# Linear attention and a feed-forward layer on one core: the seven-product second layer carried to three more groups, with a new static order

## The chip, the core and the metric

The kernel runs on one core of a Trainium2 chip. The time is the device time of one execution in microseconds (us). The engines are TensorE (PE; its weight loads are shown as PEld), VectorE (DVE), ScalarE (ACT), GpSimd (POOL) and SyncE (SP), which issues nearly all DMAs.

## What is computed

The inputs are float32: q, k and v of 8 batches, 8 heads, 576 positions and 64 columns, a 128 x 64 matrix omega, a gain of 512 and two matrices, 512 x 2048 and 2048 x 512.

```python
    scale = 1.0 / np.sqrt(np.sqrt(D))
    q_s, k_s = (q * scale, k * scale)
    def phi(x):
        proj = np.einsum('bhsd,md->bhsm', x, omega)
        sq = np.sum(x * x, axis=-1, keepdims=True) / 2.0
        h = proj - sq
        h = h - np.max(h, axis=-1, keepdims=True)
        return np.exp(h) / np.sqrt(m)
    q_p, k_p = (phi(q_s), phi(k_s))
    kv = np.einsum('bhsm,bhsd->bhmd', k_p, v)
    z = np.sum(k_p, axis=2)
    num = np.einsum('bhsm,bhmd->bhsd', q_p, kv)
    den = np.einsum('bhsm,bhm->bhs', q_p, z)[..., None] + 1e-06
    return (num / den).astype(np.float32)
...
    xn = (x - mu) / np.sqrt(var + 1e-06) * g_ln
    ch = np.maximum(xn @ w_ch1, 0.0) @ w_ch2
    return (x + ch).astype(np.float32)
```

x is that attention's result, laid out as 4608 rows (8 x 576) of 512.

## The kernel before, in words

The 4608 rows of x are 9 tiles of 512 (T), each of four chunks of 128. A float32 factor is cut into a high and a low part, so that each product is three TensorE passes (high x high, low x high, high x low). The first three tiles go through both layers in the ordinary way (`mm1`, `mm2`). The other six form three **pairs** p = 0, 1, 2, and there the first layer is done by Strassen's scheme in Winograd's form: two tiles by two blocks of 128 hidden columns take seven products instead of eight.

One pair is four **groups** (`gen_pair`). A group has two first-layer sets j (`one_set`: seven `product`, 42 matmuls of 512 columns, lines 1423 to 1425) and then the second layer of those four blocks. For pairs 0 and 1 the second layer is ordinary: eight `one_chunk`, each twelve matmuls of 512 columns (lines 1745 to 1747), whose result DVE adds into x (`drain`). For pair 2 it is two `two_chunks`, each seven `product2` of twelve matmuls of 256 columns (lines 1665 to 1667). There ACT copies and snapshots accumulators (`gen_copy`, `gen_snap`), DVE adds (`gen_x2`, `gen_y2s`) and drains by halves (`drain2`); the hidden values are first made into the seven forms A11, S3, S2, A12, S1, A22, S4, each with a low part (`form_a11` and the functions behind it, `finish`).

The seven forms of x for a pair's first layer are made by `gen_forms` (`split` writes high and low parts, `summed` the sums). They read x transposed, which `gen_flip` makes chunk by chunk by a DMA transpose: for pair 0 it goes to DRAM and back (`gen_stage`), for pairs 1 and 2 straight into one SBUF tile. The seven forms of the first weights lie in DRAM and stream through a ring of eight slots (`gen_slot`); the second weights stream through `gen_w2`, their seven forms (made by `gen_w2form`, in pair 1) through `gen_w2q_one`.

The attention's work on keys (`gen_k`, line 674), sums (`gen_sums`, line 718), queries (`gen_q`, lines 816, 833) and x (`gen_x`, line 899) is put between these matmuls as short **visits** of TensorE. The order of everything is static: while the program is built, a planner (`Plan`) with costs of its own simulates the engines and writes each engine's instructions in one fixed order. Visits are placed by the table `SLOT`, ranks shifted by `SHIFT`. In the middle layers a visit may use a pair of PSUM banks (`plan.pair`), or a second pair that is lent (`plan.loan`).

Of the kernel before, what the change touches and what calls it, by code (L numbers as in the profile page):

```python
# [23 lines left out]
P = 128  # L24
# [51 lines left out]
class Plan:  # L76
# [25 lines left out]
    def __init__(self):  # L102
# [12 lines left out]
        self.pair, self.loan, self.at, self.where = (), (), 0, 0  # L115
# [83 lines left out]
    def go_to(self, at, step):  # L199

        self.at, self.step, self.turn = at, step, 0

    def serve(self, lend):
# [11 lines left out]
        sets = (self.pair,) + (lend and len(due) > 1) * (self.loan,)  # L215
# [10 lines left out]
        if lend and len(cols) == len(todo) > 2 and guests:  # L226
# [74 lines left out]
    def run(self):  # L301
        while self.ready or self.stuck():
# [24 lines left out]
            if eng == SP:  # L327
# [6 lines left out]
                part.end = self.dma_at + (FLOWN if part.want[-1] == "flip" else 0.0)  # L334
# [12 lines left out]
def favor_ffn(ctx, tc, kT, kTr, vF, vR, qT, qD, omT, gT, w1, w2, out):  # L347
# [86 lines left out]
    def slots(pair):  # L434
        i = 512 * int(pair[0][1:])
        return all_banks.rearrange("p a b -> p (a b)")[:, i : i + H * SLOT].rearrange("p (a b) -> p a b", b=SLOT)[:, :, 0 : D + 1]

# [9 lines left out]
    n_hid, n_xnT, n_mb, n_st = names("hid", 2), names("xnT", 1), names("mb", 3), (*names("st", 3), "st3")  # L447
# [3 lines left out]
    turn = {k: names(f"turn_{k}", n) for k, n in (("k", 2), ("q", 2), ("blk", 3), ("mx", 2), ("xn", 3), ("w", 3), ("wl", 5))}  # L451
# [10 lines left out]
    plan.pair, plan.loan = b_at, b_h  # L462
# [413 lines left out]
    def gen_x(c, b_turn):  # L876
# [13 lines left out]
        t_x = yield "get", n_x  # L890
# [105 lines left out]
    def gen_flip(t, i, xn, t_n, xn_turn):  # L996
# [7 lines left out]
        if t >= NREG + 2:  # L1004
            p, u = divmod(t - NREG, 2)
            yield wait("stage", p)
            cols = slice(u * T + i * P, u * T + (i + 1) * P)
            words = stages[p][1].bitcast(U16).rearrange("p k (c b) -> p b k c", b=2)
            eng = yield either(1.27, 1.13)
            copy(eng, words[:, :, :, cols], flipped)  # L1010
            free(t_n, xn_turn, t_p)
            done(("xT", t, i))
            return
# [143 lines left out]

    n_form = ("A11", "S3", "S2", "A12", "S1", "A22", "S4")
# [6 lines left out]
    xT_away = dram.tile([P, NK, 2 * T], F32, tag="xT_away", name="xT_away", bufs=1)  # L1165
# [4 lines left out]
    hforms, fs, w2q, users, halves_left = {}, {}, {}, {}, {}  # L1170
# [61 lines left out]
    def gen_more():  # L1232
# [8 lines left out]
        extra[n_st[-1]] = more[:, 1, 0:48]  # L1241
        free(n_x[N_X + 2], n_st[-1])

    def gen_stage(p):

        if p:
            yield wait("used", 1, NF - 1)
            yield wait("formed", p - 1)
            t_s = yield "get", n_xnT
            st = tile_of(t_s, [P, NK, 2 * T])  # L1250
            stages[p] = [t_s], st
            done(("stage", p))
            return
# [9 lines left out]
        for k in range(NK):  # L1263
            plan.add(plan.cur.rank, gen_stage_k(p, k))

    def gen_stage_k(p, k):
        yield dma(P * 2 * T)
        nc.sync.dma_start(stages[p][1][k], xT_away[:, k])
# [9 lines left out]
    def gen_forms(p):  # L1278
        if p:
            for u in range(2):  # L1280
                for i in range(TC):
                    yield wait("xT", NREG + 2 * p + u, i)
        else:
            for k in range(NK):
                yield wait("xk", p, k)
# [3 lines left out]
        def cut(ap):  # L1289
            return [ap] if n_part == 1 else [ap[:, k] for k in range(2)]  # L1290
# [7 lines left out]
        def split(name, src):  # L1298
            tags, hi, lo = yield from room(name)
            for o, a in zip(cut(hi), src):  # L1300
                yield us(ACT, 0.22 + 0.00083 * 2 * T / n_part)
                nc.scalar.copy(out=o, in_=a)
            for o, a, b in zip(cut(lo), src, cut(f32(hi))):
                yield dve2(2 * T / n_part)
# [4 lines left out]
        def summed(out_, a, b, op):  # L1309
            for o, x, y in zip(out_, a, b):  # L1310
                yield dve2(2 * T / n_part)
                nc.vector.tensor_tensor(out=o, in0=x, in1=y, op=op)

        yield from split("A11", a11)
        t_s = yield "get", n_quad
        s1 = cut(tile_of(t_s, [P, 2, T]))
        yield from summed(s1, a21, a22, ALU.add)
        yield from summed(a21, a11, a21, ALU.subtract)
        yield from split("S3", a21)
        yield from summed(a11, s1, a11, ALU.subtract)  # L1320
        yield from split("S2", a11)
        yield from split("A12", a12)
        yield from split("S1", s1)
        free(t_s)
        yield from split("A22", a22)
        yield from summed(a12, a12, a11, ALU.subtract)
        yield from split("S4", a12)
        free(*stages[p][0])
        done(("formed", p))

# [34 lines left out]
    def gen_w2(p, f, t_w):  # L1365
# [6 lines left out]
        users[p, f] = 2 if p == NPAIR - 2 else 1  # L1372
        done(("w2s", p, f))

    def leave(p, f):
        users[p, f] -= 1
        if not users[p, f]:
            free(w2s[p, f][0])

    def gen_w2form(j):  # L1380
        f, g = 2 * j, 2 * j + 1
        for n in (f, g):
            yield wait("w2s", NPAIR - 2, n)
        tags = yield "get", n_big, 4
        r = [tile_of(tag, [P, DM]) for tag in tags[0:2]]
        t = [tile_of(tag, [P, 2, HALF], F32R) for tag in tags[2:4]]
        for i, n in enumerate((f, g)):
            w = f32(w2s[NPAIR - 2, n][1])
            yield dve2(DM)
# [566 lines left out]
```

## Time and profile before

| | |
|---|---|
| runs, us | 930.43, 930.6, 930.69; median 930.6 |
| profiled execution, us | 930.92 |
| its span, us | 929.2 |
| TensorE granted clock | 1.000 over the span |
| DMA | 202.71 MB, mean 218 GB/s |

In the page's parts an engine's busy time is the union of its instructions; a matmul's record lasts longer than the distance to the next one, so a busy TensorE may still issue slower than it can. The chain of work that ended last says which engine set the end. In the order's rows below, the DVE and PE instructions stand as they were written to each engine.

### The profile page before, as it was taken

The numbers are of one execution on the slowest core, as the hardware profiler recorded it, in microseconds if no ns is written. First come the engines' busy times: TensorE is split into PE (matmuls) and PEld (weight loads), VectorE is DVE, ScalarE is ACT, GpSimd is POOL, SyncE is SP. The second block draws the span as 40 slices with busy tenths as digits, with TensorE's granted clock in tenths as the row PEclk, the third lists the DMA queues.
The fourth block names the chain that finished last, engine by engine and source line by source line (L and its number), as shares of the span: only waits on it lengthen the run. The fifth ranks groups of instructions, "written<-read, shape, count | busy, mean of one in ns | idle before, by whom it ended". The sixth has DMA issues, their size and how long they took to land.

```text
span 929.2 us, 17577 instructions
## 1 busy us (share of the span) xinstructions
PE 921.2 (99%) x6871; PEld 766.9 (83%) x6871; DVE 673.6 (72%) x1178; ACT 503.1 (54%) x915; POOL 121.1 (13%) x47
## 2 busy tenths in 40 slices
PE   9999999999999999999999999999999999999998
PEld 6878777888888888888888888888888888988988
DVE  6999988674758877667566547898836596585765
ACT  7878876565753472437756444557412245253452
POOL 5001314130420041001302110304000000000000
PEclk9999999999999999999999999999999999999999
DMA  8676369996446559295956634796946558574562
GB/s 310 218 269 238 142 180 365 371 347 167 126 115 233 183 152 341 94 369 118 288 176 202 187 110 174 240 385 150 314 149 225 204 203 298 166 285 141 177 226 91
DMA packets 142577, 202.71 MB, mean 218 GB/s; under 512 B 44064, under 2 KB 79008, under 8 KB 142496
## 3 DMA queue, kind: packets, MB, share of 16 engines
q1 hardware_dynamic: 142352, 201.34, 65.6%
q8 instruction: 54, 0.88, 0.4%
q10 hardware_dynamic: 144, 0.26, 0.1%
q14 instruction: 27, 0.22, 0.1%
HBM read 140.74 MB, written 52.43 MB: 208 GB/s over the span
## 4 chain that ended last, share of the span: by engine, by line
PE 92%; DVE 6%; issue 1%; DMA 0%; SPq 0%; ACT 0%; DVEq 0%
PE b L1423 8%; PE b L1425 8%; PE b L1424 8%; PE b L1745 6%; PE b L1746 6%; PE b L1747 6%; PE b L1122 5%; PE b L1078 4%; PE b L1124 4%; PE b L1123 4%; PE b L1080 4%; PE b L1079 4%; PE b L674 4%; PE b L718 3%; PE b L899 3%; PE b L1665 3%
## 5 line engine op out<-in xcount | busy, mean ns | idle before, releaser
L845 POOL PARTITION_ALL_REDUCE quad<-quad x35 | 118.2, 3398 | 517.3 <-ACT quad L392 380.8
L1423 PE MATMUL b<-w,w 128*128 128x512 f32 x336 | 131.9, 392 | 0.0
L1425 PE MATMUL b<-w,w 128*128 128x512 f32 x336 | 130.8, 389 | 0.0
L1424 PE MATMUL b<-w,w 128*128 128x512 f32 x336 | 130.8, 389 | 0.0
L1745 PE MATMUL b<-w,w 128*128 128x512 f32 x256 | 101.2, 395 | 0.0
L1746 PE MATMUL b<-w,w 128*128 128x512 f32 x256 | 99.8, 390 | 0.0
L1747 PE MATMUL b<-w,w 128*128 128x512 f32 x256 | 99.7, 389 | 0.0
L683 ACT ACTIVATE kp<-b,mb 128x128 f32<-128x128 f32 x264 | 72.3, 389 | 26.8 <-DVE mb L677 25.9
L1122 PE MATMUL b<-w,hid 128*128 128x512 f32 x192 | 78.1, 407 | 0.0
L1078 PE MATMUL b<-xnT,w 128*128 128x512 f32 (+1 forms) x200 | 78.1, 390 | 0.0
L1080 PE MATMUL b<-xnT,w 128*128 128x512 f32 (+1 forms) x200 | 76.2, 381 | 0.0
L1079 PE MATMUL b<-xnT,w 128*128 128x512 f32 (+1 forms) x200 | 76.2, 381 | 0.0
L1124 PE MATMUL b<-w,hid 128*128 128x512 f32 x192 | 75.2, 392 | 0.8 <-DVE hid L1096 0.8
L1123 PE MATMUL b<-w,hid 128*128 128x512 f32 x192 | 75.0, 390 | 0.0
L1423 PEld LDWEIGHTS b<-w,w 128*128 128x128 f32 x336 | 63.1, 188 | 14.2 <-ACT b L1481 0.9
L1487 ACT COPY hid<-b 128x512 f32<-128x512 f32 x64 | 37.6, 587 | 68.1 <-PE b L1425 38.7
L1425 PEld LDWEIGHTS b<-w,w 128*128 128x128 f32 x336 | 63.1, 188 | 13.3
L1424 PEld LDWEIGHTS b<-w,w 128*128 128x128 f32 x336 | 63.1, 188 | 12.7
L1481 ACT COPY b<-b 128x512 f32<-128x512 f32 x32 | 18.6, 580 | 83.6 <-PE b L1425 67.8
L1494 DVE TENSOR_TENSOR b<-b,hid 128x512 f32<-128x512 f32 x32 | 22.3, 697 | 56.5 <-ACT hid L1487 56.3
L1096 DVE SCALAR_TENSOR_TENSOR hid<-b,hid 128x512 fp32r<-128x512 f32 x48 | 33.0, 688 | 37.9 <-ACT hid L1094 37.5
L1745 PEld LDWEIGHTS b<-w,w 128*128 128x128 f32 x256 | 48.0, 188 | 10.8
(220 smaller groups left out, 2050.8 us busy)
## 6 DMA issues: line engine op xcount, KB each, us to landing
w<-wf SPq DMA_DIRECT2D x168, 256.0 KB, 5.0
w<-w SPq DMA_DIRECT2D x32, 512.0 KB, 6.6
w<-w2a SPq DMA_DIRECT2D x32, 512.0 KB, 5.7
quad<-qD SPq DMA_DIRECT2D x28, 512.0 KB, 5.1
away<-x SPq DMA_DIRECT2D x33, 256.0 KB, 2.8
w2a<-w SPq DMA_DIRECT2D x16, 512.0 KB, 6.2
wf<-wide SPq DMA_DIRECT2D x32, 256.0 KB, 2.8
w2t<-wide SPq DMA_DIRECT2D x32, 256.0 KB, 3.1
```

The lines of the kernel that those rows point to most:

```text
L845: nc.gpsimd.partition_all_reduce(mx.rearrange("p a b -> p (a b)"), qc.rearrange("p a b -> p (a b)"), P, bass_isa.ReduceOp.max)
L1078: nc.tensor.matmul(ph[:, ts], w[:, 0, cs], xnT[:, 0, k, ts], start=k + i0 == 0, stop=False)
L1079: nc.tensor.matmul(ph[:, ts], w[:, 1, cs], xnT[:, 0, k, ts], start=False, stop=False)
L1080: nc.tensor.matmul(ph[:, ts], w[:, 0, cs], xnT[:, 1, k, ts], start=False, stop=k == NK - 1 and i1 == TC)
L1122: nc.tensor.matmul(accs[i][:, c], hl[:, 0, cs], w[:, 0, c], start=(f == 0), stop=False)
L1124: nc.tensor.matmul(accs[i][:, c], hl[:, 1, cs], w[:, 0, c], start=False, stop=f == NF - 1 and c == parts[-1])
L1423: nc.tensor.matmul(o, w[:, 0, cs], hi[:, k], start=first and k == 0, stop=False, skip_group_check=True)
L1424: nc.tensor.matmul(o, w[:, 1, cs], hi[:, k], start=False, stop=False, skip_group_check=True)
L1425: nc.tensor.matmul(o, w[:, 0, cs], lo[:, k], start=False, stop=k == 1, skip_group_check=True)
L1745: nc.tensor.matmul(acc[:, o], hl[:, 0, cs], w[:, 0, o], start=n == 0 and o is parts[0], stop=False)
L1746: nc.tensor.matmul(acc[:, o], hl[:, 0, cs], w[:, 1, o], start=False, stop=False)
L1747: nc.tensor.matmul(acc[:, o], hl[:, 1, cs], w[:, 0, o], start=False, stop=n == 3 and o is parts[-1])
```

## The change

Four things change together. (1) `strassen2` says that groups 1 to 3 of pair 1 (`G1` = 1) also take the seven-product second layer; all hidden forms and weight loads get the pair as an index. (2) `gen_w2form` no longer waits for pair 1's own loads of the second weights: it reads them from DRAM itself (`gen_w2in`) after chunk 19 of x. (3) x transposed goes through DRAM for all three pairs, so that the SBUF tile can hold up to eight more chunks of x (`n_room`, `lend_room`) until a pair is staged; the forms of x are made by parts that run side by side. (4) Visits in the pairs may use a third pair of banks, the two accumulators alternate over all sets (`turned`), and the tables of the static order are all new.

```diff
-        sets = (self.pair,) + (lend and len(due) > 1) * (self.loan,)
+        sets = (self.pair,) + self.where * (self.third,) + (lend and (len(due) > 1 or self.where > 0)) * (self.loan,)
...
+        if t >= ORDERED:
+            yield wait("place", c - 1)
-        t_x = yield "get", n_x
+        t_x = yield "get", n_x + n_room
...
-        if t >= NREG + 2:
-            p, u = divmod(t - NREG, 2)
-            yield wait("stage", p)
...
-            copy(eng, words[:, :, :, cols], flipped)
...
-                xT_away[:, :, u * T + i * P : u * T + (i + 1) * P], f32(whole).rearrange("p (a b) c -> p a (b c)", b=P)
+                xT_away[u // 2][:, :, u % 2 * T + i * P : u % 2 * T + (i + 1) * P], f32(whole).rearrange("p (a b) c -> p a (b c)", b=P)
...
     def gen_stage(p):
         if p:
-            yield wait("used", 1, NF - 1)
             yield wait("formed", p - 1)
-            t_s = yield "get", n_xnT
-            st = tile_of(t_s, [P, NK, 2 * T])
+            yield wait("a2b", p - 1, STAGE[p - 1][0])
+            for n in n_room:
+                yield "get", (n,)
+            for u in range(2):
+                for i in range(TC):
+                    yield wait("xT", NREG + 2 * p + u, i)
+            st = tile_of(n_xnT[0], [P, NK, 2 * T])
...
+            for k in range(NK):
+                plan.add(plan.cur.rank, gen_stage_k(p, k, st[:, k]))
...
+    def gen_stage_k(p, k, place):
+        if p:
+            yield wait("a2b", p - 1, STAGE[p - 1][k])
         yield dma(P * 2 * T)
-        nc.sync.dma_start(stages[p][1][k], xT_away[:, k])
+        nc.sync.dma_start(place, xT_away[p][:, k])
...
+        if p:
+            yield wait("a2b", p - 1, FORM_AT if p < 2 else FORM_LAST)
+        def begin(name, src):
+            plan.add(rank + n_form.index(name), split(name, src))
+        begin("A11", a11)
+        begin("A12", a12)
+        begin("A22", a22)
...
+    def strassen2(p, gr):
+        return p == NPAIR - 1 or (p == NPAIR - 2 and gr >= G1)
...
     def gen_w2form(j):
-        f, g = 2 * j, 2 * j + 1
-        for n in (f, g):
-            yield wait("w2s", NPAIR - 2, n)
+        yield wait("x", W2GO)
+        for n in (2 * j, 2 * j + 1):
+            yield wait("w2", n)
...
+        for i in range(2):
+            plan.add(plan.cur.rank, gen_w2in(2 * j + i, r[i], low[i]))
...
+    def gen_w2in(f, r, low):
+        yield dma(2 * P * DM, 0.5)
+        nc.sync.dma_start(r, w2_away[f][:, 0])
+        nc.sync.dma_start(low, w2_away[f][:, 1])
+        done(("w2in", f))
...
+    def turned():
+        other = b_acc[1 - b_acc.index(latest[0])]
+        b_c, latest[0] = latest[0], other
+        return other, b_c
...
+    def two_chunks(p, gr, h):
+        ta, j = NREG + 2 * p, NF + 2 * gr + h
+        b_a, b_d = b_acc[2:4] if h else b_at
+        b_b, b_c = turned()
...
-            if p == NPAIR - 1:
+            if strassen2(p, gr):
                 for h in range(2):
-                    yield from two_chunks(gr, h)
+                    yield from two_chunks(p, gr, h)
                 continue
...
-W2F = -30
+G1 = 1
+ORDERED = 7
+STAGE, FORM_AT, FORM_LAST = ((2, 3, 4, 5), (4, 5, 6, 6)), 7, 22
+W2GO = 19
+W2F = (240, 25)
```

`SHIFT`, `SLOT`, `EARLIER`, `WF` and some planner constants have other numbers; three places show what they and the code do to the order.

**TensorE, end of the first-layer sets of pair 1's second group.** Before (lines 1423 to 1425 are the last product of the set, 1745 to 1747 the first ordinary chunk):

```order
L1423 MATMUL b<-w_100_6139,w_10_3495 128x512
L1424 MATMUL b<-w_100_6139,w_10_3495 128x512
L1425 MATMUL b<-w_90_6140,w_10_3495 128x512
L1745 MATMUL b<-w_100_6727,w_130_6813 128x512
L1746 MATMUL b<-w_100_6727,w_130_6813 128x512
L1747 MATMUL b<-w_100_6727,w_130_6813 128x512
L1745 MATMUL b<-w_120_6734,w_150_6876 128x512
```

Of the change, at the same place (lines 1716 to 1718 are `product2`):

```order
L1460 MATMUL b<-w_100_6513,w_10_3489 128x512
L1461 MATMUL b<-w_100_6513,w_10_3489 128x512
L1462 MATMUL b<-w_90_6514,w_10_3489 128x512
L1716 MATMUL b<-w_100_7014,kp_7079 128x256
L1717 MATMUL b<-w_100_7014,kp_7079 128x256
L1718 MATMUL b<-w_100_7014,kp_7079 128x256
```

In three groups 96 matmuls of 512 columns become 168 of 256: over the program, `one_chunk` has 480 instead of 768, `product2` 1176 instead of 672.

**TensorE, the last visits.** Before, `gen_x` (line 899) stands by itself inside a first-layer set of pair 1's second group:

```order
L1424 MATMUL b<-w_50_5990,w_110_4033 128x512
L1425 MATMUL b<-w_40_5991,w_110_4033 128x512
L899 MATMUL b<-kv_5257,quad_6634 64x65 x16
L1423 MATMUL b<-w_60_6057,w_00_3410 128x512
L1424 MATMUL b<-w_60_6057,w_00_3410 128x512
```

Of the change, two `gen_x` (line 902) stand together ahead of pair 1's first group's chunks (1800 to 1802 are `one_chunk`):

```order
L1461 MATMUL b<-w_100_6513,w_20_3593 128x512
L1462 MATMUL b<-w_90_6514,w_20_3593 128x512
L902 MATMUL b<-kv_5160,quad_6630 64x65 x16
L902 MATMUL b<-kv_5160,quad_6635 64x65 x16
L1800 MATMUL b<-w_100_6582,w_130_6673 128x512
L1801 MATMUL b<-w_100_6582,w_130_6673 128x512
```

Behind the first matmul of `mm1` the order has 64 stretches of visits before and 59 now, with the same matmuls in them; the last visit is in pair 1's second group before, and in its first group now.

**DVE, end of pair 1**, where the forms of x for pair 2 are made. Before, among the chunks (1305 `split`, 1312 `summed`, 1765 `drain`, 1390 to 1402 `gen_w2form`):

```order
L1305 TENSOR_TENSOR w_40_7533<-xnT_6190,w_50_7532 128x1024
L1765 SCALAR_TENSOR_TENSOR x_6384<-b,w_150_4372,x_6384 128x512
L1312 TENSOR_TENSOR xnT_6190<-quad_7504,xnT_6190 128x2x512
L1402 TENSOR_TENSOR wide_7427<-wide_7427,wide_7566 128x512
L1390 TENSOR_TENSOR wide_7474<-w_120_7395 128x512
L1765 SCALAR_TENSOR_TENSOR w_150_4372<-b,w_150_4372 128x512
L1305 TENSOR_TENSOR w_50_7582<-xnT_6190,w_60_7581 128x1024
```

Of the change, among the two sets of `two_chunks` (1306 `split`, 1313 `summed`, 1538 `gen_x2`, 1773 `drain2`):

```order
L1773 SCALAR_TENSOR_TENSOR w_150_4353<-b,w_150_4353 128x256
L1313 TENSOR_TENSOR xnT_7437<-xnT_7437 128x2x512
L1773 SCALAR_TENSOR_TENSOR x_6729<-b,w_150_4353,x_6729 128x256
L1306 TENSOR_TENSOR w_30_8019<-xnT_7437,w_40_8018 128x1024
L1306 TENSOR_TENSOR w_60_8021<-xnT_7437,w_70_8020 128x1024
L1313 TENSOR_TENSOR xnT_7437<-wide_8024,xnT_7437 128x512
L1306 TENSOR_TENSOR w_40_8135<-xnT_7437,w_50_8134 128x1024
L1538 TENSOR_TENSOR b<-b,hid_4359 128x512
L1773 SCALAR_TENSOR_TENSOR x_6740<-b,w_150_4353,x_6740 128x256
L1313 TENSOR_TENSOR xnT_7437<-wide_8025,xnT_7437 128x512
```

The forms' DVE work now stands in front of the second set's `gen_x2`, on which TensorE waits; the weights' forms are gone from here, to earlier places.

## Rows read from the trace of the kernel before

**Rows 1.** The page: part 1, and engines of the chain in part 4.
```profile
PE 921.2 (99%) x6871; PEld 766.9 (83%) x6871; DVE 673.6 (72%) x1178; ACT 503.1 (54%) x915; POOL 121.1 (13%) x47
PE 92%; DVE 6%; issue 1%; DMA 0%; SPq 0%; ACT 0%; DVEq 0%
```
**Rows 2.** Timeline of PE (start us, us, engine, line): rows with idle before, in brackets.
```profile
39.48 0.50 PE L1124 MATMUL b<-w,hid 128*128 128x512 f32 x1 [0.29 <-DVE hid L1096]
128.15 0.49 PE L1124 MATMUL b<-w,hid 128*128 128x512 f32 x1 [0.54 <-DVE hid L1096]
151.84 0.50 PE L833 MATMUL b<-quad,om_hi 128*128 128x512 f32 x1 [0.46 <-DVE kv L746]
484.95 0.47 PE L833 MATMUL b<-quad,om_hi 128*128 128x512 f32 x1 [0.16 <-DVE x L910]
```
**Rows 3.** Windows: one second layer of pair 1, then of pair 2; columns ahead.
```profile
core 0: us, PE busy (x) PEld busy (x) DVE busy (x) ACT busy (x) POOL busy (x), PEclk, DMA share, GB/s
704.96:726.72 21.76, 21.76 (x98) 18.02 (x96) 9.86 (x17) 1.22 (x2) 0.00 (x0) 1.00 0.33 115
865.40:885.45 20.05, 20.05 (x170) 20.04 (x169) 13.77 (x28) 6.73 (x12) 0.00 (x0) 1.00 0.29 108
```
**Rows 4.** Timeline of PE: matmuls of 512 columns, then of 256.
```profile
710.17 0.39 PE L1747 MATMUL b<-w,w 128*128 128x512 f32 x1
710.40 0.39 PE L1745 MATMUL b<-w,w 128*128 128x512 f32 x1
...
870.08 0.28 PE L1665 MATMUL b<-w,w 128*128 128x256 f32 x1
870.20 0.28 PE L1666 MATMUL b<-w,w 128*128 128x256 f32 x1
```
**Rows 5.** The chain of waits, two visits (start us, us, what): double, single.
```profile
410.75 2.02 PE b L899 x64
412.76 0.43 PE b L1745
...
446.20 1.08 PE b L899 x32
447.28 0.43 PE b L1423
```
**Rows 6.** Timeline of DVE: pair 1's end, then pair 2's first second layer.
```profile
747.97 1.22 DVE L1305 TENSOR_TENSOR w<-xnT,w 128x1024 fp32r<-128x1024 f32 x1
749.11 0.74 DVE L1765 SCALAR_TENSOR_TENSOR x<-b,w,x 128x512 f32<-128x512 f32 x1
...
788.69 0.68 DVE L1606 SCALAR_TENSOR_TENSOR wide<-b,wide 128x512 f32<-128x512 f32 x1
789.29 0.68 DVE L1534 TENSOR_TENSOR quad<-wide,quad 128x512 fp32r<-128x512 f32 x1
...
798.32 0.48 DVE L1719 SCALAR_TENSOR_TENSOR w<-hid,st,w 128x256 f32<-128x256 f32 x1
798.71 0.48 DVE L1719 SCALAR_TENSOR_TENSOR w<-b,st,w 128x256 f32<-128x256 f32 x1
...
802.16 0.70 DVE L1494 TENSOR_TENSOR b<-b,hid 128x512 f32<-128x512 f32 x1 [2.19 <-ACT hid L1487]
```
**Rows 7.** Timeline of PE: the first matmul of that second layer.
```profile
786.68 0.28 PE L1665 MATMUL b<-w,kp 128*128 128x256 f32 x1
```
**Rows 8.** Windows: pair 0's first two groups, pair 1's first, a stretch early on.
```profile
388.80:440.40 51.60, 51.60 (x410) 42.81 (x409) 34.47 (x58) 27.28 (x55) 3.23 (x1) 1.00 0.79 254
440.40:498.80 58.40, 58.24 (x505) 47.68 (x504) 37.17 (x69) 38.38 (x72) 12.90 (x4) 1.00 0.68 208
593.00:642.50 49.50, 49.50 (x325) 40.46 (x324) 46.10 (x75) 31.14 (x42) 17.48 (x5) 1.00 0.85 276
139.00:209.00 70.00, 69.55 (x651) 55.78 (x651) 54.06 (x97) 44.57 (x80) 19.86 (x6) 1.00 1.08 359
```
**Rows 9.** One line's instructions: the ring's loads, L1353.
```profile
DMA to landing us min/median/max: 2.6/5.0/8.1
```

More of the change, by code (lines that the diff above doesn't have):

```diff
@@ L114, in __init__ @@
         self.mlp = None
-        self.pair, self.loan, self.at, self.where = (), (), 0, 0
+        self.pair, self.loan, self.third, self.at, self.where, self.zone = (), (), (), 0, 0, 0
         self.shared = {}
@@ L225, in serve @@
         guests = [p for p in cols if p.want[3]]
-        if lend and len(cols) == len(todo) > 2 and guests:
+        if lend and not self.where and len(cols) == len(todo) > 2 and guests:
             todo.remove(guests[0])
@@ L1475, in one_set @@
         tick(6)
-        plan.add(MOST_URGENT, form_a12(j, b_b) if wide else relu2(ta, g, bank(b_b), b_b))
+        plan.add(MOST_URGENT, form_a12(p, j, b_b) if wide else relu2(ta, g, bank(b_b), b_b))
     def gen_copy(p, j, b_a, b_b):
@@ L1544, in form_a11, with form_a22 @@
         free(b_a)
-        done(("f", j, "A11"))
-        yield from finish(j, "A11")
-    def form_a22(j, s):
-        a22 = yield from whole(j, "A22")
+        done(("f", p, j, "A11"))
+        yield from finish(p, j, "A11")
+    def form_a22(p, j, s):
+        a22 = yield from whole(p, j, "A22")
         eng = yield either(0.5, 0.34)
@@ L1595, in form_a12 @@
         )
[L1596 removed]
+        done(("hf", p, j, "A12"))
         left_b.pop()
@@ L1611, in form_s4 @@
             free(b_b)
-        done(("f", j, "S4"))
+        done(("f", p, j, "S4"))
         plan.cur.rank = MOST_URGENT
-        yield from finish(j, "S4")
+        yield from finish(p, j, "S4")
     def gen_w2q():
@@ L1659, in product2 @@
             w = w2q[t_w]
-            for i in range(2):
-                o = bank(t_b)[:, i * HALF : (i + 1) * HALF]
-                cs = slice((2 * h + i) * P, (2 * h + i + 1) * P)
-                yield us(PE, 0.36)
-                fresh, last = first and i == s == 0, s == 1
-                nc.tensor.matmul(o, hl[:, 0, cs], w[:, 0], start=fresh, stop=False, skip_group_check=True)
-                nc.tensor.matmul(o, hl[:, 0, cs], w[:, 1], start=False, stop=False, skip_group_check=True)
-                nc.tensor.matmul(o, hl[:, 1, cs], w[:, 0], start=False, stop=last, skip_group_check=True)
@@ new lines, in product2 @@
+            nc.tensor.matmul(o, hl[:, 0, cs], w[:, 0], start=fresh, stop=False, skip_group_check=True)
+            nc.tensor.matmul(o, hl[:, 0, cs], w[:, 1], start=False, stop=False, skip_group_check=True)
+            nc.tensor.matmul(o, hl[:, 1, cs], w[:, 0], start=False, stop=last, skip_group_check=True)
+            if h and i:
+                free(tag, t_w)
+    def two_chunks(p, gr, h):
+        ta, j = NREG + 2 * p, NF + 2 * gr + h
+        b_a, b_d = b_acc[2:4] if h else b_at
+        b_b, b_c = turned()
+        sk = snaps[h]
```

312 lines of the change are left out of this document (164 added, 148 removed).

## The prediction, made before the changed kernel was run

> **What bounds the kernel now.** I read the page first: TensorE is busy 99% of the span, and 92% of the chain that ended last is TensorE [rows 1]. Busy time alone would not prove it, so I then looked in the timeline for every row of TensorE with idle time before it. After the first 32 us only four waits are long enough to be marked, 0.29, 0.54, 0.46 and 0.16 us, 1.45 together [rows 2]: three for DVE on the way to hidden values, queries or a sum, one for DVE on x. The kernel is bound by the number of matmuls that TensorE issues, from 32 us to 4 us before the end. A change gains only by taking issues away, and it loses as soon as any other engine or a DMA is late.
>
> The clock is granted at 1.00, that is 2.4 GHz, in all stretches shown [rows 3, 8], and TensorE has no long pauses in which it could fall; I leave it out.
>
> **Seven products for eight.** Before, the second layer of a quiet group of pair 1 takes 21.76 us; the same work in pair 2, done with seven products, takes 20.05 us [rows 3]. Both windows run from the stage's first matmul to that of the next stage, and hold no visit. They are 96 matmuls at 0.227 us (start to start: 710.17 to 710.40) and 168 at 0.12 (870.08 to 870.20) [rows 4]. The three groups that change are of just this kind, so the term is 3 x 1.71 = **5.1 us gained**. The extra matmuls, 504 for 288, are already in it. Half as many columns take 53% of the time, not 50%, so of the eighth that is saved in columns (12.5%) 7.9% remains.
>
> Here the Trainium skill speaks another way. "TensorE: Matmul & The Clock Gate", section "Back-to-back issue gap", gives a warm gap of N/2.4 + 2.5 ns. By it the gain would be an estimated 288 x 215.8 - 504 x 109.2 ns = 7.1 us, 2 us more than by the rows; no matmul of rows 4 is that quick, so the measured windows decide.
>
> **Visits.** The order has 59 stretches of visits for 64. What a stretch costs beyond its own matmuls shows in the chain: a single `gen_x` takes 1.08 us and the matmul behind it 0.43; two in one stretch take 2.02 and again 0.43 [rows 5]. A free matmul takes 0.23 [rows 4]. Two single ones cost 2 x (1.08 + 0.20) = 2.56 us, a double one 2.02 + 0.20 = 2.22. Each joined pair saves 0.34 us, and five save **1.7 us**. The work in them is the same. Other mixes (keys beside x) save a little less, so 1.2 to 1.7.
>
> **DVE's new work.** From the order: 36 more `finish`, 18 `form_sum`, 6 each of `form_s4`, `form_a12`, `form_a22`, `gen_x2` and `gen_y2s`, 48 `drain2`; 24 `relu2` and 24 `drain` fewer. DVE issues 512 columns every 0.60 us, a `drain2` every 0.39 and 1024 columns every 1.14 us [rows 6]. With `form_a22` at a `drain2`'s price, 78 x 0.60 + 54 x 0.39 less 48 x 0.60 is about 39 us more work. It costs nothing where DVE has time: the same second layer in pair 2 leaves DVE idle 6.3 of 20 us [rows 3], and none of TensorE's waits [rows 2] lies there. Without that cover each late `gen_x2` would stop TensorE by as much as it is late.
>
> **The seam of pair 1 and 2** is where cover is thinnest. Eleven operations of 1024 columns for pair 2's forms of x (four sums, seven low parts; some cut in two) are 11 x 1.14 = 12.5 us. They had eight ordinary chunks (21.8 us) with one `drain` each; now they share 20 us with 10 us of drains and sums. I laid the DVE order out from the start of the second layer. The last set's `form_s4` starts 2.0 us after that (786.68 to 788.69) [rows 6, 7]. From there to the start of the second set's `gen_x2` stand 11 operations of 512 columns (6.6 us), 8 drains (3.1), a cast (0.3) and 4 of 1024 (4.6): it starts at +16.6 and ends at +17.3. Today its twin starts at +15.5 (802.16) [rows 6], after idling for ACT. TensorE needs it for the second set's sixth product, at 10.0 + 5 x 1.44 = +17.2. So it is some 0.1 us late. The low part of S2 then ends at about +23.9; pair 2's third product wants it at 20.05 + 2 x 1.36 + 0.45 = +23.2: another 0.7 us. **Cost 0.8 us**; bounds 0 (a tenth faster per operation) and 3 us (as much again from each of the three forms that follow).
>
> **Moved at no cost.** `gen_w2form` (eight times four operations of 512 and four of 256 columns, some 4 us each time [rows 6]) leaves pair 1, where DVE was busy 46.1 of 49.5 us in the first group [rows 8] without holding TensorE, for earlier groups. Pair 0's first two groups have DVE busy 71.6 of 110 us [rows 8]. By the order three of the eight `gen_w2form`, nine more `gen_q` steps and more of x come in, and their DVE work rises by half, to about 100 us of a stretch that visits lengthen to 117. That is 0.87, less than the 0.93 that went well. The waits of rows 2 may go or others come: I keep their 1.45 us and take 0 and twice that as bounds. The start (up to 32 us) has the same TensorE matmuls, and the last group the same instructions: nothing.
>
> **DMAs.** In: 16 stores of x transposed, 8 loads of it (512 KB), 32 `gen_w2in` and 42 loads of weight forms, 256 KB each; out: 12 `gen_w2` of 512 KB. Net some 21 MB on 203. SP takes them in order, so a store that waits for its drain holds what is queued behind it; at the end of pair 1 these are 15 stores. What must not be late are the ring's loads. They land 2.6 to 8.1 us after their issue [rows 9], and eight slots at 1.36 us a product give 10.9 us. No cost.
>
> **Sum.** 930.92 (profiled execution; span 929.2) - 5.1 - 1.7 + 0.8 = 924.9. The median of the runs stands 0.3 us below the profiled execution, so the forecast is **924.6 us**.
>
> **Rivals.**
> *DVE sets the pace* (0.10). If DVE is late not once but in each new wide group and in pair 0's full stretch, TensorE loses 0.5 to 1 us in some six places, and the gain falls to 2 or 3 us: 928. For it speaks that DVE's share in pair 0 rises to 0.87; against it that 0.93 cost nothing in pair 1 and that pair 2's groups carry the same wide work without a wait.
>
> *The DMA queue in pair 0* (0.06, slower). Counted between ring loads in SP's order, pair 0's first two groups move about 36 MB where they moved 23. The ring of weights then waits behind transposes, `gen_w2in` and stores, and TensorE's `product` waits for its slot. 36 MB in 117 us is 308 GB/s. For it: in today's first group the queue is 0.79 busy at 254 GB/s [rows 8], which at a full share would be 321. Against it: 359 GB/s were held for 70 us earlier [rows 8]. It decides below about 285 GB/s: 36 MB then take 126 us, 9 us too many, and the time is some 933. By the Trainium skill, "DMA: Bandwidth & Descriptors", section "Where 436 GB/s comes from", the core's HBM limit is about 358 GB/s; the 359 of rows 8 agree with that, and by it this rival stays out.
>
> *Weight loads bind* (0.01). Each 256-column matmul has its own weight load; the loads fill 20.04 of 20.05 us there, against 18.02 of 21.76 [rows 3]. If they could not run beside matmuls the groups would be slower than the ordinary ones, but rows 3 have that cost in them.
>
> *The order gives nothing back* (0.08). The three groups save 5.1 us, but the joined visits end on later data and their 1.7 us go into new waits: 926.5.
>
> **How the numbers follow.** The forecast has 0.75. Its own range is 922.3 (no seam, the old waits gone: 924.6 - 0.8 - 1.45) to 928.2 (seam 3 us, the waits doubled: 924.6 + 2.2 + 1.45). For 8 in 10 the range takes in most of the DVE case above and is rounded down below: 922.0 to 928.5. A change under 0.2% (1.9 us) can hardly be told from none, so "faster" ends at 928.7. The forecast, the visits case and six tenths of the DVE case lie under it, with little of the forecast's own tail beyond: 0.85. The rest of the DVE case and that tail are "same", 0.09; the DMA case is "slower", 0.06.
>
> **What would show it.** Right: the wide second layers of pair 1 at 20.0 to 20.2 us; TensorE's marked waits 1 to 3 us in all; a wait of 0.5 to 1 us in pair 2's first set, released by DVE's `split`. The visits are wrong if a joined pair still costs two times 1.28 us. The forecast falls if TensorE has waits ended by a DMA into w (the ring), if landings pass 10.9 us in pair 0, or if wide groups of pair 1 take over 21 us.

## The result and the profile after

The changed kernel took 935.52 us (median of 934.68, 935.53, 935.52 and 937.79) against 930.62: 1.0051 times as long, 95% interval 1.0039 to 1.0064. It is slower by 0.5%, where 924.6 was forecast. Measured again in rounds with the kernel before it was 934.88 to 930.97, with a ratio on record of 1.0067 (1.0040 to 1.0094); the two medians alone give 1.0042, and two long runs of the six, 940.33 and 942.15, raise the ratio. The profiled execution took 937.79 and was the slowest of the first four; its span is 936.0 us, 6.8 more than before.

The page's part 1 and the engines of the chain [rows 1 before]:

```profile
PE 920.0 (98%) x7087; PEld 775.0 (83%) x7087; DVE 706.8 (76%) x1278; ACT 522.7 (56%) x959; POOL 118.2 (13%) x47
PE 84%; DVE 10%; ACT 2%; DMA 2%; issue 1%; SPq 0%; DVEq 0%; ACTq 0%
```

TensorE has fallen from 92% to 84% of the chain; DVE has risen from 6% to 10%, ACT and DMA from 0% to 2% each. The windows, with columns as in rows 3: the first and the third wide second layer of pair 1; two short stretches; the two stretches of time of pair 0 that rows 8 show; and pair 0's first two groups as they lie in the changed kernel:

```profile
675.46:695.50 20.04, 20.04 (x169) 20.03 (x168) 13.76 (x28) 6.72 (x12) 0.00 (x0) 1.00 0.34 124
...
753.92:774.25 20.33, 20.33 (x170) 20.15 (x168) 20.30 (x36) 12.00 (x18) 0.00 (x0) 1.00 0.58 208
...
471.46:474.87 3.41, 3.41 (x35) 2.92 (x32) 2.35 (x9) 0.00 (x0) 3.05 (x1) 0.50 1.03 414
522.66:526.07 3.41, 3.41 (x9) 2.67 (x8) 1.27 (x2) 0.73 (x2) 0.00 (x0) 0.50 1.09 298
388.80:440.40 51.60, 51.60 (x514) 42.81 (x514) 43.31 (x73) 30.44 (x64) 9.64 (x3) 1.00 1.01 335
440.40:498.80 58.40, 56.08 (x545) 45.95 (x543) 47.18 (x92) 37.74 (x66) 14.24 (x5) 0.97 0.94 283
...
387.20:516.69 129.49, 126.93 (x1205) 104.20 (x1204) 108.57 (x194) 82.93 (x151) 33.51 (x10) 0.99 0.97 293
```

The seven products are worth nearly what was said: 20.04 us, 20.33 in the third group, for 21.76 [rows 3]. But twice the granted clock is 0.50, that is 1.2 GHz, for 3.41 us, about half of which, 1.7 us, is lost each time; before, it was 1.00 in every stretch read. In the two stretches of rows 8 the DMA engines are busy 1.01 and 0.94 of the time, for 0.79 and 0.68. Pair 0's first two groups now last 129.5 us, where the prediction had 117; over them DVE is busy 0.84 of the time, and the DMA engines 0.97 at 293 GB/s. TensorE's waits, summed by the pair of lines (us in total, times, longest):

```profile
PE b L1460 <- ACT b L1525: 2.3, 1, 2.3
PE b L902 <- ACT quad L392: 1.8, 1, 1.8
...
PE b L1460 <- ACT hid L1531: 1.1, 1, 1.1
PE b L674 <- DVE x L913: 1.0, 2, 0.6
PE b L674 <- ACT kp L683: 0.9, 1, 0.9
PE b L1115 <- ACT hid L1087: 0.7, 1, 0.7
PE b L1117 <- DVE hid L1089: 0.6, 2, 0.3
PE b L718 <- ACT quad L392: 0.5, 1, 0.5
```

With two short ones (L1462 0.3, L833 0.2) that is 9.4 us behind the first 32 us, where four waits of 1.45 us in all stood [rows 2]; the three longest end on ACT. The timeline of PE at those three, called the three stops below, with the first matmuls at the halved clock, and at the seam of pair 1 and 2:

```profile
471.18 1.80 PE L902 MATMUL b<-kv,quad 128*64 128x65 f32 x32 [1.77 <-ACT quad L392]
472.91 0.80 PE L1460 MATMUL b<-w,w 128*128 128x512 f32 x1
...
521.87 0.50 PE L1460 MATMUL b<-w,w 128*128 128x512 f32 x1 [2.29 <-ACT b L1525]
522.20 0.39 PE L1461 MATMUL b<-w,w 128*128 128x512 f32 x1
522.43 0.43 PE L1462 MATMUL b<-w,w 128*128 128x512 f32 x1
522.67 0.63 PE L1460 MATMUL b<-w,w 128*128 128x512 f32 x1
...
617.27 0.50 PE L1460 MATMUL b<-w,w 128*128 128x512 f32 x1 [1.14 <-ACT hid L1531]
...
777.91 0.50 PE L1462 MATMUL b<-w,w 128*128 128x512 f32 x1 [0.29 <-DVE w L1306]
```

And the timeline of ACT there, which says why ACT was late:

```profile
467.22 1.05 ACT L1003 COPY wide<-wide 128x1024 uint16<-128x1024 uint16 x1 [1.87 <-DMA xTa<-wide]
468.17 0.59 ACT L1554 ACTIVATE w<-b 128x512 fp32r<-128x512 f32 x1
468.66 0.59 ACT L1525 COPY b<-b 128x512 f32<-128x512 f32 x1
469.17 1.05 ACT L853 ACTIVATE quad<-quad 128x1024 f32<-128x1024 f32 x1
470.13 1.00 ACT L392 COPY quad<-b 128x1024 f32<-128x1024 f32 x1
...
513.87 1.09 ACT L1003 COPY wide<-wide 128x1024 uint16<-128x1024 uint16 x1
519.04 1.05 ACT L1003 COPY wide<-wide 128x1024 uint16<-128x1024 uint16 x1 [4.09 <-DMA w2t<-wide]
520.00 1.34 ACT L392 COPY wide<-wide 128x1024 uint16<-128x1024 uint16 x1
521.19 0.62 ACT L1525 COPY b<-b 128x512 f32<-128x512 f32 x1
...
616.03 0.72 ACT L986 ACTIVATE wide<-w,w 128x512 f32<-128x512 f32 x1 [2.23 <-DMA w2t<-wide]
616.66 0.56 ACT L1531 COPY hid<-b 128x512 f32<-128x512 f32 x1
```

At 513.87 ACT starts the word split (`gen_flip`, L1003) of one chunk, and then comes to the next chunk's. Its output goes into one of eight `wide` buffers, whose last user is a store of the second weights' forms (`w2t<-wide`) that has not landed. ACT sits idle for 4.09 us. Two places behind the word split stands `gen_copy` (L1525), for which TensorE waits 2.29 us. The other two places read the same way, one with a store of x transposed (`xTa<-wide`). By the Trainium skill, "PSUM — Partial Sum Buffer", section "Engine vs sequencer instructions", the queues of ScalarE, VectorE and GpSimd are strict FIFO; the rows of ACT agree. The page's part 6 has the store's landing, before and after (KB, median us):

```profile
w2t<-wide SPq DMA_DIRECT2D x32, 256.0 KB, 3.1
```
```profile
w2t<-wide SPq DMA_DIRECT2D x32, 256.0 KB, 5.2
```

**Where the time went.** I took each matmul's distance to the next start in the timeline and subtracted what that pair of shapes takes when nothing waits. What is left over, TensorE's lost time, is 12.2 us before and 26.2 after. So issuing changed by 936.0 - 929.2 - 14.0 = -7.2 us, near the forecast's -6.8, and 14.0 us of stalls ate it twice over: 5.7 us in the three stops (1.96, 2.45, 1.30 from start to start), 3.4 in the clock behind two of them, 4.9 in some ten smaller ones. The count depends somewhat on what is taken as free: with the median distance of each pair of shapes in these traces the rise is 13 us, and issuing fell by some 6 us.

### The profile page after: what moved, and what is told of

The parts are those of the page before. It is cut to its first block, busy times and chain, and to the rows that moved or that the text cites. A ratio compares the mean times of both kernels' runs of the same rounds, so it can differ in the third digit from the quotient of the medians.

```text
span 936.0 us, 18335 instructions
## 1 busy us (share of the span) xinstructions
PE 920.0 (98%) x7087; PEld 775.0 (83%) x7087; DVE 706.8 (76%) x1278; ACT 522.7 (56%) x959; POOL 118.2 (13%) x47
## 2 busy tenths in 40 slices
DMA packets 164567, 224.28 MB, mean 240 GB/s; under 512 B 45568, under 2 KB 95360, under 8 KB 164480
## 4 chain that ended last, share of the span: by engine, by line
PE 84%; DVE 10%; ACT 2%; DMA 2%; issue 1%; SPq 0%; DVEq 0%; ACTq 0%
PE b L1460 8%; PE b L1462 8%; PE b L1461 8%; PE b L1071 5%; PE b L1115 4%; PE b L1718 4%; PE b L1717 4%; PE b L1716 4%; PE b L1117 4%; PE b L1116 4%; PE b L1072 4%; PE b L1073 4%; PE b L718 4%; PE b L674 4%; PE b L1800 3%; PE b L902 3%
## 5 line engine op out<-in xcount | busy, mean ns | idle before, releaser
L845 POOL PARTITION_ALL_REDUCE quad<-quad x35 | 115.3, 3318 | 500.4 <-ACT quad L392 281.4
L1460 PE MATMUL b<-w,w 128*128 128x512 f32 x336 | 134.2, 399 | 3.4 <-ACT b L1525 2.3
L1462 PE MATMUL b<-w,w 128*128 128x512 f32 x336 | 131.9, 392 | 0.3 <-DVE w L1306 0.3
L1461 PE MATMUL b<-w,w 128*128 128x512 f32 x336 | 131.9, 392 | 0.0
L1531 ACT COPY hid<-b 128x512 f32<-128x512 f32 x76 | 44.8, 590 | 85.9 <-PE b L1718 45.8
L683 ACT ACTIVATE kp<-b,mb 128x128 f32<-128x128 f32 x264 | 74.3, 394 | 21.6 <-DVE mb L677 21.2
L1460 PEld LDWEIGHTS b<-w,w 128*128 128x128 f32 x336 | 63.6, 189 | 19.4 <-ACT b L1525 4.3
L1462 PEld LDWEIGHTS b<-w,w 128*128 128x128 f32 x336 | 63.7, 190 | 14.5 <-DVE w L1306 0.7
L1538 DVE TENSOR_TENSOR b<-b,hid 128x512 f32<-128x512 f32 x38 | 26.4, 696 | 63.3 <-ACT hid L1531 63.3
L1461 PEld LDWEIGHTS b<-w,w 128*128 128x128 f32 x336 | 63.8, 190 | 12.4
L1800 PE MATMUL b<-w,w 128*128 128x512 f32 x160 | 63.3, 396 | 0.0
L1801 PE MATMUL b<-w,w 128*128 128x512 f32 x160 | 62.4, 390 | 0.0
L1802 PE MATMUL b<-w,w 128*128 128x512 f32 x160 | 62.3, 389 | 0.0
L1525 ACT COPY b<-b 128x512 f32<-128x512 f32 x38 | 22.0, 579 | 69.2 <-PE b L1462 43.1
L677 DVE TENSOR_REDUCE mb<-b 128x8 f32<-128x1024 f32 x36 | 43.5, 1217 | 12.4 <-PE b L674 12.2
```

Source lines behind the costliest of these rows:

```text
L683: nc.scalar.activation(out=kp[:, j], in_=pk[:, s, j % 4], func=AF.Exp, scale=1.0, bias=mb[:, j : j + 1])
L845: nc.gpsimd.partition_all_reduce(mx.rearrange("p a b -> p (a b)"), qc.rearrange("p a b -> p (a b)"), P, bass_isa.ReduceOp.max)
L1460: nc.tensor.matmul(o, w[:, 0, cs], hi[:, k], start=first and k == 0, stop=False, skip_group_check=True)
L1461: nc.tensor.matmul(o, w[:, 1, cs], hi[:, k], start=False, stop=False, skip_group_check=True)
L1462: nc.tensor.matmul(o, w[:, 0, cs], lo[:, k], start=False, stop=k == 1, skip_group_check=True)
L1800: nc.tensor.matmul(acc[:, o], hl[:, 0, cs], w[:, 0, o], start=n == 0 and o is parts[0], stop=False)
```

## The experiments

The theory: ACT's order is written for stores that land sooner than they do; where one is late, ACT's queue and then TensorE stand still. Rivals: DVE's larger load sets the pace; the DMA traffic as such does. Lost time below is that of the profiled execution, taken as above. One execution need not be typical: in e5, e10 and e12 the profiled one was the fastest of its runs, in e2 the slowest.

| run | median us (lowest to highest) | to before, 95% interval | lost, us |
|---|---|---|---|
| e1_three_later | 931.93 (931.2 to 934.7) | 1.0011 (1.0002, 1.0020) | 20.2 |
| e2_one_later | 934.11 (930.8 to 937.2) | 1.0031 (1.0019, 1.0043) | 24.4 |
| e3_store_prices | 938.22 (936.7 to 939.6) | 1.0075 (1.0061, 1.0089) | 25.0 |
| e4_no_form_stores | 931.39 (929.5 to 934.4) | 1.0006 (0.9995, 1.0016) | 18.3 |
| e5_more_later | 932.15 (930.7 to 934.7) | 1.0017 (1.0008, 1.0026) | 18.2 |
| e6_act_stores | 932.17 (930.0 to 934.1) | 1.0011 (1.0003, 1.0020) | 18.4 |
| e7_no_form_work | 934.09 (931.2 to 937.8) | 1.0034 (1.0023, 1.0046) | 20.8 |
| e8_no_store | 929.80 (928.3 to 931.0) | 0.9982 (0.9973, 0.9991) | 18.7 |
| e9_ordinary_pair1 | 941.85 (938.8 to 944.4) | 1.0112 (1.0091, 1.0133) | 22.9 |
| e10_both | 932.80 (929.9 to 934.0) | 1.0014 (1.0004, 1.0023) | 18.0 |
| e11_new_order | 928.48 (927.7 to 929.2) | 0.9973 (0.9962, 0.9983) | 15.4 |
| e12_changed_again | 934.88 (933.7 to 942.2) | 1.0067 (1.0040, 1.0094) | 21.6 |

The kernel before, in the same rounds: medians 930.95 to 931.06, 930.2 to 932.5 in all. e12 is the changed kernel itself:

> The changed kernel itself once more, beside the kernel before in the same rounds: 934.5 to 938, with a scatter of 3 us or more from run to run, as against the kernel before's 1.8, if late stores, whose landing differs from run to run, set its stalls; a scatter under 1.8 us would speak for stalls that the order alone makes.

It was as expected, and scattered by 8.5 us; its three stops were 0.96, 1.41 and 1.71 us in this profile, and the clock stayed at 1.00 behind them. So they are not fixed in length.

**Three ACT instructions later (e1), one later (e2).** The planner decides as before; ACT's instruction is written to its queue some places later. The orders of PE, DVE, POOL and SP are unchanged.

```diff
+LATER_BY = {('flip', 25): 4, ('flip', 30): 2, ('xn', 32): 1}
...
-        nc.scalar.copy(out=halves, in_=xn.bitcast(U16).rearrange("p (a b) -> p b a", b=2))
+        plan.later("flip", c, lambda: nc.scalar.copy(out=halves, in_=xn.bitcast(U16).rearrange("p (a b) -> p b a", b=2)))
```

> The changed kernel with three ACT instructions issued a few places later and nothing else moved: the word split of chunk 25 behind four others, that of chunk 30 behind two, the normalisation of chunk 32 behind one. In the changed kernel's trace each of them waits for a buffer whose store to DRAM has not landed, and TensorE's three longest stalls (1.96, 2.45 and 1.30 us, 5.7 in all) wait for the ACT instruction queued right behind. Theory (ACT's in-order queue, held by late stores): the three stalls go, and with them the fall of the clock that followed (1.7 us in a usual run, 3.4 in the profiled one); 935.5 - 5.7 - 1.7 = 928.1, between 926.5 and 930. Rival (DVE's larger load sets the pace, and the stalls only show where it is collected): the time comes back within the next groups as other stalls, 933 to 936. Rival (DMA traffic as such): the same, 933 to 936.

> Only chunk 30's word split is moved, behind two ACT instructions. Theory: the 2.45 us stall goes, the other two stay; 933.1 if the clock's fall stays with another stall, 931.4 if the fall belongs to this one, and in the profile no half clock at 522.7 us. Rivals (DVE's pace, DMA traffic): 934 to 936.

In e1's timeline of ACT `gen_copy` (L1550 there) now stands ahead of the word split (L1029), and waits for TensorE, not TensorE for it:

```profile
516.45 0.57 ACT L1550 COPY b<-b 128x512 f32<-128x512 f32 x1 [1.98 <-PE b L1487]
516.93 1.05 ACT L1029 COPY wide<-wide 128x1024 uint16<-128x1024 uint16 x1
```

The first two stops are gone, the third is down to 0.52 us, and the clock is 1.00. But 931.9 is some 2 us above the theory's range, and 1 us below the rivals': stops of 0.79, 0.41, 0.56 and 0.48 us stand at 498, 506, 513 and 530 us (the one at 513 was 0.40 in the changed kernel). In e2 the stop at 519 us is gone and no clock falls there; the one at 612 us is 2.62 us in that profile, with a fall behind it. Its median of 934.11 is 1 us above the theory's 933.1 and lies in the rivals' range. Theory and rival each have a part: the order makes the long stops, and something gives part of it back.

**Without the stores (e4).** In the same order `gen_w2put` issues no store.

```diff
-        nc.sync.dma_start(w2t_away[j][:, 2 * i : 2 * i + 2, k], f32(src))
...
-            nc.sync.dma_start(w, w2t_away[j][:, (1, 2, 4, 5).index(q)])
+            nc.sync.dma_start(w, wf_away[j][:, q])
```

> The changed kernel's order with the 32 stores of the second weights' forms left out, and their loads reading other data of the same size; so the wide second layers use other weights. Theory (a buffer freed by a late store holds ACT): the two stalls that end on such a store go (2.45 and 1.30 us), the one that ends on a store of x transposed stays (1.96); 935.5 - 3.75 = 931.8, or 930.1 if a clock fall goes too. Rival (DVE's pace): no change in the stalls, 934.5 to 936, since DVE has the same work. Rival (DMA traffic as such): 8 of 224 MB less, a gain of under 1 us, 934.5 to 935.5.

The two stops that end on such a store are gone; the one on x transposed was 0.45 us here. 931.4 is close to the theory's 931.8; both rivals' ranges begin at 934.5, above the highest of its ten runs. The traffic fell with the stores here, by 8 of 224 MB; e11 below keeps it.

**Without the forms' arithmetic (e7).** Loads and stores stay; the ten additions, subtractions and casts of each `gen_w2form` go.

> The changed kernel's order with the DVE and ACT work of the second weights' forms left out: their loads and stores stay, and store what was loaded (so the wide second layers use other weights). DVE has some 27 us less work between 420 and 640 us, and 16 ACT or DVE casts go. If DVE's load sets the pace there, all stalls of pair 0 shrink: 928 to 931. If the stores' landing is what counts, the stalls that end on them stay, since the same stores go out: 932 to 936; somewhat better than 935.5, because stores that needn't wait for DVE are issued as soon as SP comes to them.

The waits of TensorE, in this kernel's lines:

```profile
PE b L1456 <- ACT hid L1527: 1.3, 1, 1.3
...
PE b L902 <- ACT quad L392: 0.9, 1, 0.9
PE b L1456 <- ACT b L1521: 0.7, 1, 0.7
```

The same three stops (1.09, 0.90 and 1.46 us from start to start), and 934.1 us, in the range written down for the stores. So DVE's load by the forms does not make the stops.

**Without any of the added stores (e8).** No work, loads or stores for the weights' forms, no stores of x transposed for pairs 1 and 2 (`u < 2 and nc.sync.dma_start` in `gen_flip`).

> As the kernel without the forms' work, and in addition without their loads and stores (16 MB) and without the 16 stores of x transposed for pairs 1 and 2 (their forms are made from pair 0's): no buffer in the pairs is freed by a late store any more, in the same order on PE and ACT. Theory: the stalls of pair 0 go, but for the one that is ACT's own order (0.74 at 458 us) and the 0.4 at 513; those before pair 0 stay (0.46, 1.1, 0.46, 0.68, 0.85, 0.46: 4.0 us) because they are in the order of ACT and DVE. The time is 927.5 to 929.5, and from run to run it scatters by under 1.5 us, where the runs with all stores scatter by 3.5 to 4. If the order as such stalls TensorE in pair 0 without any late store, 931 or more.

929.8, 0.3 above the range, 5.1 below e12, and a scatter of 2.6 us for e12's 8.5 (under 1.5 was expected). In pair 0 0.74 and 0.14 us of stops are left. Two us were lost in pair 1 on its own loads, which read another array than they should:

```profile
PE b L1712 <- DMA v<-wf: 0.9, 1, 0.9
...
PE b L1712 <- DMA kv<-wf: 0.6, 2, 0.4
```

Ahead of pair 0 the stops stay as said, 4.0 us. The run leaves out the added traffic and the forms' work too; what it shows by itself is that the same order on PE and ACT holds no long stop in pair 0 without them.

**The stores issued by ACT (e6).** `nc.scalar.dma_start` in `gen_w2put`.

> The changed kernel with the 32 stores of the second weights' forms issued by ACT in place of SP, so that they pass through another DMA queue and not behind SP's transposes and loads; the order is otherwise the same. If the stores are late because of what stands ahead of them in SP's queue, they land in about 3 us, where the changed kernel's trace has a median of 5.2, and the stalls that end on them (2.45 and 1.30 us) shrink below 0.5 each; against it ACT, in order, now waits for DVE's subtraction ahead of each store, some 0.6 us at up to 16 places. 930 to 935. If they are late because the DMA engines are full, they land after 5 us as before and the stalls stay: 935 to 938.

The landing of those stores, e6:

```profile
DMA to landing us min/median/max: 2.1/5.3/8.0
```

By the median they land no sooner. By the Trainium skill, "DMA: Bandwidth & Descriptors", section "Issuing engines are not separate DMA queues", DMAs of all issuing engines run on the same 16 DMA engines; 5.3 against 5.2 us agrees. The stops are gone in the profile nevertheless, and the time fell to 932.2. A median of 32 says little of the few stores that hold ACT. The store that ended ACT's 4.09 us, in the changed kernel and then in e6:

```profile
510.49 1.44 SPq L1006 DMA_TRANSPOSE wide<-wide  x1
511.97 1.13 SPq L1445 DMA_DIRECT2D w2t<-wide  x2
```
```profile
507.82 0.37 ACTq L1445 DMA_DIRECT2D w2t<-wide  x1
```

In the changed kernel its data were ready by 507.3 us, where the cast on ACT (L392) ends; SP had other DMAs to issue first, came to it at 511.97, and it landed 7.0 us later. In e6 the cast ended at 505.5, the issue came at 507.82, and it landed after 3.8 us. At the third stop the two casts end at 609.0 us at the latest and SP issues at 610.26, in e6 one ends at 602.3 and ACT issues at 602.35; the landing is the same there (5.7 and 5.9 us), and ACT's wait falls from 2.23 to 0.58 us. So a store is late in two ways, by its place in SP's order and by its landing, and the first has a part in these stops.

**More moves (e5), and both (e10).** Ten more moves on ACT and DVE, and six of them with ACT's stores.

> The changed kernel with the three moved ACT instructions of the first experiment (chunk 32's two now behind the next relu as well) and ten more small moves on ACT and DVE, each putting an instruction on which nothing of TensorE hangs behind one that TensorE waits for: for example the cast of query 28 behind the copy that frees a bank for a sum (0.74 us of stall in the trace of the first experiment), the statistics of chunk 14 behind chunk 15's last step (0.68), the exponentials of a key block behind the relu of the next hidden block (0.85 and 0.47), a weight cast behind the exponentials of the first key block (0.55 of 1.05), the statistics of chunk 30 behind a query's step (0.41), one form of the second weights behind a sum (0.79), one that waits for its load behind the first set's addition (0.5). PE's, POOL's and SP's order and all work stay. Theory (the order of ACT and DVE is what went wrong, stall by stall): 5.0 us less than the 931.9 of the first experiment, 926.9, between 925.5 and 929, and so under the kernel before. Rival (what is won at one place is lost at the next, since DVE's or the DMAs' load sets the pace): 930 to 933.

> The changed kernel with the forms' stores issued by ACT and the moves of ACT and DVE instructions of the earlier experiments, without those three before pair 0 that won nothing there. From the 932.2 of the kernel with ACT's stores, the moves should take the stalls at 271.9 (0.5 of 0.68), 459.5 (0.75 of 0.96) and 512.8 (0.41): 930.5, between 929 and 932. If what is won is lost at the next late DMA, as in the second set of moves, 932 to 933.

Both missed, and both medians lie in the range written down for the rival, that what is won at one place is lost at the next. In e5 the stops at 458, 498, 513 and 613 us fell as planned (0.74 to 0.21, 0.52 to 0.30 at 613, the other two gone), but 0.59 us came at 72, 0.60 at 95, 0.92 at 304, 0.38 at 280; in e10 the 0.85 at 277 us became 1.27, and 0.64 came at 525. The profiled spans are 928.8 and 928.2, while the medians of all runs stay at 932 to 933. Moving single instructions round a stop helped in the profiled execution and not in the usual one. That the landings move from run to run would explain it; only the profiled executions show landings, so it is not shown.

**The ordinary second layer in pair 1 (e9).** `G1 = 4`; TensorE's order is the same up to the second layer of pair 1's second group.

> The changed kernel with the ordinary second layer in all four groups of pair 1 (and the forms of x for pair 2 after pair 1's last first-layer set); up to there the order of TensorE is the same, stalls included. If the seven products are worth what the windows say, 3 x 1.71 us more, less the 0.45 at the seam: 935.5 + 4.7 = 940.2, between 938.5 and 942. If the wide groups give nothing in this kernel, 935 to 937.

941.85: the seven products are worth 7.0 us by the medians of e9 and e12, 5.6 by the profiles without their lost time (938.8 - 22.9 less 931.9 - 21.6), and 4.2 by the two ratios (1.0112 less 1.0067). The term of 5.1 lies among these, so it holds inside the changed kernel.

**Prices and a new order (e3, e11).** Two numbers of the planner, then also its tables.

```diff
-            yield dma(P * DM, -0.4)
+            yield dma(P * DM, 0.2)
...
-        yield dma(2 * P * HALF, -0.85)
+        yield dma(2 * P * HALF, 1.75)
...
-W2GO = 19
-W2F = (240, 25)
+W2GO = 18
+W2F = (1400, 69)
```

The first two edits are e3. In e11 296 of `SHIFT`'s entries, 46 of `SLOT`'s, `STAGE` and `EARLIER` differ as well, and the forms of groups 0 and 1 wait for chunk 20.

> The planner's price for two kinds of stores: those of the second weights' forms land 2.6 us later by it, those of x transposed 0.6 us later, near the 5.2 and 3.7 us medians of the changed kernel's trace. The whole order is planned anew, but the table of visits is the same. Theory (the plan took these stores to land too soon): ACT's waits for stores fall from 14 us to under 5, and the time to 927 to 932. Rival (DVE's pace): no better than the changed kernel, 934 to 938. A new order may also bring stalls of its own, so a time above 932 tells less than one below.

> The same work as the changed kernel, with the two kinds of stores priced in the planner as landing 2.6 and 0.6 us later (as in the run with the stores' prices alone) and the tables of the order (visits, ranks, begin and spacing of the second weights' forms) searched again under these prices. Theory (the order was made for stores that land sooner than they do; seven products and joined visits are worth 6.8 us where no store is late): the stalls of 1 us and more in pair 0 go, and with them the clock's falls; from the changed kernel's 935.5 at least the 5.7 us of stalls and 1.7 us of clock: 928, and if the stalls ahead of pair 0 shrink too, down to the forecast's 925; 924.5 to 929. Rival (pair 0 carries more DVE work and DMA traffic than it can hide, whatever the order): 931 to 936, with new stalls in the trace.

e3 missed by 6 us: it has stops of 1.66, 1.00, 1.95, 1.96 and 1.52 us at other places (458 to 609 us). That the old table of visits does not fit the new prices is the likely reason, not a shown one. e11, with the same work and the same 224.28 MB, is faster than the kernel before by 0.27%. Its longest waits of TensorE, and ACT's for stores:

```profile
PE b L519 <- DVE spin L478: 1.2, 1, 1.2
PE b L1115 <- ACT hid L1087: 0.7, 1, 0.7
PE b L1117 <- DVE hid L1089: 0.6, 2, 0.3
PE b L816 <- DVE hid L1089: 0.5, 1, 0.5
```
```profile
ACT wide L1003 <- DMA w2t<-wide: 7.2, 2, 4.5
...
ACT wide L986 <- DMA xTa<-wide: 3.1, 1, 3.1
```

ACT still waits up to 4.5 us for a store. TensorE doesn't notice, because nothing that it needs stands close behind (L519 lies within the first 32 us). Pair 0 carries as much as in the changed kernel, DVE 88.0 us for 90.5 and the DMA engines as full:

```profile
388.80:440.40 51.60, 51.36 (x513) 42.42 (x514) 39.63 (x71) 31.48 (x65) 9.86 (x3) 1.00 1.00 344
440.40:498.80 58.40, 58.40 (x594) 47.71 (x591) 48.32 (x97) 42.95 (x70) 15.97 (x5) 1.00 0.97 294
```

This decides between theory and rivals: load and traffic are those of the changed kernel, the order is not. Which of the many new entries does it is not shown; the two prices alone (e3) did not. And from run to run it scatters by 1.6 us.

## Why the prediction was wrong

- **What bounds the kernel**: right, and with it the warning that any late engine or DMA costs at once.
- **Seven products, 5.1 us**: right. The three second layers take 65.3 us before and 20.05 + 20.04 + 20.33 = 60.4 now, 4.9 us less; e9 agrees. The 7.1 by the Trainium skill ("TensorE: Matmul & The Clock Gate", section "Back-to-back issue gap", whose formula is for the isolated gap) is not reached in any window.
- **Visits, 1.7 us**: too much; about 1 us. Visits with the matmul behind them, added up from start to start without stops over 0.25 us, take 115.2 us before, 114.5 in the changed kernel's profile and 114.0 in e12. That is five times the 0.20 us behind a stretch; the other 0.14 us of a joined pair did not show. The 64 and 59 stretches leave out those of `gen_q` at lines 833 and 834 (with them the traces have 92 and 81), whose matmuls follow at 0.23 us like any other.
- **DVE's new work at nothing**: right as far as was tried. e7 takes the forms' part away and gains 0.8 us by the medians on e12, inside the scatter; by the ratios (1.0034 and 1.0067) it could be more. Two wide groups hold at 20.04 and 20.05, the third loses 0.3.
- **The seam, 0.8 us**: right in place and engine (L1306, `split`), half in size: 0.45 us from start to start, and no wait for the second set's `gen_x2`.
- **"Moved at no cost"** is the step that failed. It priced the moved `gen_w2form` by DVE's busy share alone, kept the 1.45 us of rows 2 and took "0 and twice that as bounds". What moved with it are 32 stores of 256 KB, from pair 1 (614 to 765 us) to pair 0 and the start of pair 1 (421 to 639 us, 24 of them in pair 0), each holding one of eight `wide` buffers until it lands, and users of these buffers stand in ACT's queue. Lost time rose by 14.0 us in the profiled execution, 9.1 of them in the three stops and the clock. By medians the added stores with their work and traffic are worth 5.1 us (e12 less e8), or some 7 with the 2 us that e8 lost on its own loads, of the 10.9 that the forecast missed by.
- The same sentence let the old waits stand for the whole new order, and that failed a second time: ahead of 388 us, before the first of these stores, stops over 0.3 us add up to 4.1 us, for 1.8 before (the 0.52 at L816, the same in both, left out). They wait for ACT and DVE, and e4, e7 and e8 leave them as they are; which part of the change makes them was not tried.
- **"DMAs. No cost"** failed in the same place: it asked only whether the ring's loads are late. They are not (2.7 to 9.1 us, under the 10.9); the stores are, 5.2 for 3.1 us from issue to landing, and by SP's order besides (e6). That a landing store also sets when a buffer comes free was not asked.
- **The clock, "I leave it out"**: followed from having no long pauses, and fell with it: 3.4 us in the profiled execution, nothing in e12's.
- **Rivals**: the DMA queue in pair 0 (933) had the place and the full DMA engines (0.97 busy at 293 GB/s, near the 285 that it named; the 359 of the earlier stretch was no measure for this one), but the wrong victim: no wait of TensorE there ends on the ring. 0.06 was far too little. DVE's pace is excluded by e7 and e11. The order that gives nothing back had the right subject, but allowed new waits only the visits' 1.7 us.
- The sign hung on the order's tables: e11 shows the change's parts worth -2.5 us with another order, at the edge of the range. In its profile the lost time is still 3.2 us above the kernel before, among it stops of 0.3 to 0.85 us ahead of pair 0; with the 0.7 us that the visits lack, that is most of what keeps it from 924.6.

## What to carry to other kernels

When work moves into a stretch, list its stores with the buffers that they hold, and for each buffer the next user and what stands behind that user in its engine's queue; an engine's busy share says nothing of this. Price a store by its place in the issuing engine's order and its landing in the stretch that it moves to, not in the one that it comes from. And judge a static order by several executions: one profile can show a stop at its shortest.

## What the runs showed that was not expected

- The granted clock fell from 1.00 to 0.50 for 3.41 us behind stops of 1.96 and 2.45 us in the changed kernel and of 2.62 in e2, and not behind stops of 1.95, 1.96 (e3) and 1.98 us (e9). What else decides is open. A fall costs some 1.7 us, nearly as much as the stop.
- The forms' stores, 32 of 256 KB, land in 5.2 us (median) in the changed kernel and in 2.8 in e11:

```profile
w2t<-wide SPq DMA_DIRECT2D x32, 256.0 KB, 2.8
```

They are issued in the same part of the program (421 to 639 us, and 421 to 647), with as much traffic in all. What is in flight beside them would explain it; it was not tried, and neither was which neighbour it is.
